# A delta rule and a gated MLP on one core: masks to GpSimd, both grams in one tile, the opening re-ordered, the lanes dealt by TensorE's load

## The chip, the cores and the metric

The kernel runs on one core of a Trainium2 chip. A core has engines that run side by side, each in the order of its own instruction queue: TensorE (PE in the profile; its weight load is PEld), which multiplies matrices into the accumulators PSUM; VectorE (DVE) and ScalarE (ACT), which work element by element and read PSUM; GpSimd (POOL), here used on SBUF alone; and SyncE (SP), which issues most of the DMAs. One engine waits for another by semaphores. The metric is the device time of one execution in microseconds (us), lower is better.

## The reference: what is computed

Inputs are q, k, v of shape (4 batches, 8 heads, 768 steps, 48) and beta (4, 8, 768), all float32, and the weights of a gated MLP. The first half is a recurrence over time, one state of 48 x 48 for each batch and head:

```python
k_n = k / (norm(k, axis=-1) + 1e-6)
state = 0
for t in range(768):
    y[t] = q[t] @ state
    v_old = state.T @ k_n[t]
    state = state + beta[t] * outer(k_n[t], v[t] - v_old)
```

The output y, with its heads side by side, is x of shape (4, 768, 384). The second half is

```python
h = gelu_tanh(x @ w_in)                 # 384 -> 1024
u, v = h[..., :512], h[..., 512:]
v_n = (v - mean(v)) / sqrt(var(v) + 1e-6) * g_ln
v_s = einsum('ts,bsd->btd', w_sg, v_n) + b_sg[:, None]   # mixes the 768 steps
out = x + (u * v_s) @ w_out
```

## The kernel before

**The recurrence in chunks.** Time is cut into 12 chunks of 64 steps (`NCH`, `T`), and six segments of two chunks (`NSEG`). The 32 pairs of batch and head lie as 16 pairs on each half of the partitions. For a chunk, TensorE makes two grams, keys by keys (G) and keys by queries (M). M is masked so that only earlier steps count. From G comes a triangular matrix that must be inverted, Z: its two 32 x 32 diagonal blocks are inverted element by element with 128 blocks side by side, one on each partition (`lanes`, line 301), and the off-diagonal corner is then multiplied together on TensorE (`corner_a`, `corner_b`, lines 435 to 465).

**The lanes.** `gstore` (229) writes G to device memory, `zload` (294) reads a segment's blocks back as `z`. `lanes(s)` gives two lists: `first` (a copy of the diagonal d0 at line 315, a GpSimd select that clears the lower triangle at 316, three Newton steps for 1/sqrt and what follows) and `ops` (a scaling at 338, then rows at 344, outer products and sums at 355 and 362, columns at 349, and a last scaling at 381), all on VectorE. `zstore` (401) writes the result out, makes a transposed copy of half of it on ScalarE (410), writes that too, and its `fetch` reads both back in the layout that TensorE needs, 16 DMAs in all. All these DMAs stand in SP's queue, in program order.

**The chain.** For each chunk c the dictionary of `chain(c)` (504) holds eight steps: `own0/1` (u from Z and v), `old0/1` (less what the state already holds), `state0/1` (the state's update) and `read0/1` (the output), where 0 and 1 are halves of the pairs. Into `old` and `state` the grams of chunk c + 5 are dealt (`gram`, 266; `AHEAD = 5`), into `read` the `keys` (467) of chunk c + 1. `old` opens on a flag: a one-element GpSimd memset (520) that waits for the last matmul of `own`, and for which `old`'s first matmul waits. The values v of a chunk are multiplied by a factor from the keys' norms in `vprep` (489), and `norms` (387) brings those norms into place.

**The MLP.** From chunk 2 on, `Ffn(c - 2)` works on the chunk that is two behind: `turn` (665) transposes x and splits it into a high and a low part (`xh` on ScalarE, `xl` on VectorE, line 678), `value` and `gate` are three matmuls for each product (`mm3`, 648), `moments` (691) and `norm` (696) are the layer norm's sums on VectorE, `scale` and `ustore` finish and store. The weights w_in are float64 words that `decode` (590) takes apart into a high and a low part in three steps `one`, `two`, `three`; there are six blocks of w_in (`decode_win`, 630), which must all be ready before the first `value`. The words of a block come by a DMA on GpSimd's queue (`win_load`, 623). The late weights (w_out by the same `decode`, w_sg by a split) are prepared from chunk 10 on.

**The order.** The engines' order is written out by hand. `tick` (153) takes an operation from the list `bg` (the lanes, later the late weights) and one from `slow`; `tick(n)` calls stand between the steps of the loop over chunks (812 to 945), with fixed numbers. At the end of each even chunk the loop empties what is left of a segment's lanes, stores it, and starts the next list. Before chunk 2 all remaining w_in blocks are decoded in one go (815). After chunk 13 the hand-written order ends, and the last stage (`spatial`, 976; `project`, 995) mixes the steps and projects.

**The opening** (740 to 810): loads of the k and q halves of chunks 0 and 1, keys' grams, q grams, one w_in block in two steps, grams of chunks 2 and 3, lanes(0) in one go, store and fetch, masks, the gram of chunk 4 after the first corner.

**The masks and the factor before:** a ScalarE copy of G out of PSUM, and one VectorE multiplication of M by a constant mask on its way out of PSUM (258, 286); the factor is a VectorE multiplication (492).

## Time and profile before

| what | value |
|---|---|
| time, median of 3 runs | 643.38 us (642.31 to 646.55) |
| the profiled execution, its own time | 636.94 us |
| its span | 634.9 us |
| TensorE, VectorE, ScalarE, GpSimd busy | 471.0, 360.1, 198.1, 66.0 us |
| granted TensorE clock, mean | 0.836 |
| HBM traffic | 55.94 MB read, 29.88 MB written |

All rows below come from one profiled execution, times in us from the start of its span. The profile's chain of waits gives the last stage's matmuls (lines 651 to 653) 27% of the span. A row of a timeline is: start, duration, engine, line, operation, output<-inputs, shape, count, and in brackets how long the engine had been idle and what ended that. A row of a group is: line, engine, operation, tiles, shape, count, then busy us, mean ns of one, and idle us before them with what ended it. A row of stages is explained where it stands.

### The profile page before, as it was taken

Reading aid. Unit: us, or ns where it says so; the run is one execution under the profiler, and the core shown is the slowest. Engines: PE = TensorE matmul, PEld = TensorE weight load, DVE = VectorE, ACT = ScalarE, POOL = GpSimd, SP = SyncE. Lnnn points to the kernel's source line nnn. Section 1 sums busy time; section 2 is a strip of 40 time slices with the busy share of each in tenths; the row PEclk is TensorE's granted clock in tenths of the full one; section 3 lists DMA queues with packets and bytes.
Section 4 is the critical chain, followed back from the end, with each engine's and each line's share of the span. In section 5 each row is a group of like instructions: output and inputs, shape, how many; then the busy total and the mean of one; then the engine's idle time right before and its main releaser. Section 6 shows DMA issues by size and latency. Waiting matters only on the chain. (4 is left out here: it accounts for less than half of the span.)

```text
span 634.9 us, 20005 instructions
## 1 busy us (share of the span) xinstructions
PE 471.0 (74%) x8530; PEld 424.1 (67%) x8531; DVE 360.1 (57%) x1295; ACT 198.1 (31%) x426; POOL 66.0 (10%) x98
## 2 busy tenths in 40 slices
PE   8355656340779595979599691738969999999997
PEld 6352555330567584768488581527859999999997
DVE  1695769878466359647866622753342763633332
ACT  2101213221263435345254451145442331311100
POOL 3100100023000000000000000200000422222210
PEclk9658667675798588879699896777979999999999
DMA  8746864771076957774755655245394664432123
GB/s 157 147 84 167 173 113 118 128 177 66 26 174 128 209 123 180 143 171 104 195 118 149 160 127 138 88 141 140 73 274 118 229 214 152 154 112 93 41 74 113
DMA packets 124872, 87.12 MB, mean 137 GB/s; under 512 B 94352, under 2 KB 110352, under 8 KB 123824
## 3 DMA queue, kind: packets, MB, share of 16 engines
q1 hardware_dynamic: 118336, 81.56, 51.6%
q0 software_dynamic: 864, 3.15, 1.7%
q10 hardware_dynamic: 5584, 1.15, 1.2%
q8 instruction: 67, 1.10, 0.8%
q14 instruction: 21, 0.17, 0.1%
HBM read 55.94 MB, written 29.88 MB: 135 GB/s over the span
## 5 line engine op out<-in xcount | busy, mean ns | idle before, releaser
L72 PE MATMUL ps<-kd 48*64 48x64 f32 (+1 forms) x1024 | 69.9, 306 | 30.2 <-DMA kd<-kqT 28.9
L651 PE MATMUL ps<-winh,xh 128*128 128x512 f32 x72 | 36.2, 503 | 66.4 <-DVE xl L678 56.5
L72 PEld LDWEIGHTS ps<-kd 48*64 48x64 f32 x1024 | 62.1, 182 | 33.4 <-DVE ztmp L355 13.6
L651 PEld LDWEIGHTS ps<-winh,xh 128*128 128x128 f32 x72 | 16.3, 227 | 71.3 <-DVE xl L678 44.1
L355 DVE TENSOR_TENSOR ztmp<-zl 128x72 f32<-128x72 f32 (+13 forms) x228 | 51.6, 262 | 1.5
L362 DVE TENSOR_TENSOR zl<-zl,ztmp 128x72 f32<-128x72 f32 (+13 forms) x228 | 51.0, 260 | 0.0
L988 POOL TENSOR_TENSOR ga<-ga,uT 128x384 f32<-128x384 f32 x32 | 34.4, 1079 | 144.9 <-DVE ga L986 94.8
L72 PE MATMUL ps<-z,kt 64*64 64x64 f32 x704 | 33.0, 260 | 17.3 <-DVE zl L362 9.2
L651 PE MATMUL ps<-xh,winh 128*128 128x256 f32 x144 | 45.3, 314 | 0.4 <-ACT vg L689 0.4
L656 ACT CAST gh<-ga 128x384 fp32r<-128x384 f32 x32 | 16.4, 513 | 86.0 <-POOL ga L988 86.0
L72 PEld LDWEIGHTS ps<-z,kt 64*64 64x64 f32 x704 | 30.1, 171 | 18.1 <-issue 17.6
L652 PE MATMUL ps<-xl,winh 128*128 128x256 f32 x144 | 41.4, 287 | 0.3 <-issue 0.3
L653 PE MATMUL ps<-xh,winl 128*128 128x256 f32 x144 | 41.3, 287 | 0.0
L657 DVE TENSOR_TENSOR gl<-ga,gh 128x384 fp32r<-128x384 f32 x32 | 18.9, 592 | 32.0 <-ACT gh L656 32.0
L286 DVE TENSOR_TENSOR mq<-ps,mask 128x256 f32<-128x256 f32 x32 | 13.5, 422 | 37.6 <-ACT g L285 37.5
L72 PE MATMUL ps<-u,mq 64*64 64x48 f32 x768 | 34.4, 253 | 0.0
L693 DVE BATCH_NORM_STATS2 bs<-vg 128x6 f32<-128x512 f32 x24 | 16.4, 685 | 31.2 <-ACT vg L689 31.2
L651 PEld LDWEIGHTS ps<-xh,winh 128*128 128x128 f32 x144 | 28.2, 196 | 8.2 <-issue 5.4
L652 PE MATMUL ps<-winl,xh 128*128 128x512 f32 x72 | 33.6, 467 | 0.0
L72 PEld LDWEIGHTS ps<-s,w 48*64 48x64 f32 x704 | 25.8, 153 | 11.4 <-issue 5.1
L653 PE MATMUL ps<-winh,xl 128*128 128x512 f32 x72 | 33.4, 464 | 0.0
L72 PEld LDWEIGHTS ps<-u,mq 64*64 64x64 f32 x768 | 31.3, 168 | 2.5 <-issue 1.5
(125 smaller groups left out, 1264.9 us busy)
## 6 DMA issues: line engine op xcount, KB each, us to landing
kd<-kqT SPq DMA_DIRECT2D x20, 384.0 KB, 6.3
vD<-vg SPq DMA_DIRECT2D x48, 128.0 KB, 2.5
uD<-ut SPq DMA_DIRECT2D x48, 128.0 KB, 3.2
vraw<-vD SPq DMA_DIRECT2D x24, 256.0 KB, 3.8
uT<-uD SPq DMA_DIRECT2D x8, 768.0 KB, 5.5
kt<-ktok SPq DMA_DIRECT2D x12, 384.0 KB, 3.8
v<-vtok SPq DMA_DIRECT2D x12, 384.0 KB, 4.3
xD<-x SPq DMA_DIRECT2D x48, 96.0 KB, 2.7
```

The lines of the kernel that those rows point to most:

```text
L72: return nc.tensor.matmul(out=out, lhsT=lhsT, rhs=rhs, start=start, stop=stop, skip_group_check=True)
L286: nc.vector.tensor_tensor(out=M[c % N_M][:, js], in0=st["ps"][:, :, 1], in1=mask.unsqueeze(1).broadcast_to([P, 4, T]), op=ALU.mult)
L355: tv.tensor_tensor(out=st["tmp"][:, at:at + (r1 - r0) * w].rearrange("p (r t) -> p r t", t=w), in0=z[:, r0:r1, i:i + 1].broadcast_to([P, r ...
L362: tv.tensor_tensor(out=z[:, r0:r1, i + 1:32], in0=z[:, r0:r1, i + 1:32], in1=st["tmp"][:, at:at + (r1 - r0) * w].rearrange("p (r t) -> p r ...
L651: nc.tensor.matmul(out=ps, lhsT=sh, rhs=mh, start=(first and i == 0), stop=False)
L652: nc.tensor.matmul(out=ps, lhsT=sh, rhs=ml, start=False, stop=False)
L653: nc.tensor.matmul(out=ps, lhsT=sl, rhs=mh, start=False, stop=(last and i == n - 1))
L656: nc.scalar.copy(out=hi, in_=src)
L657: nc.vector.tensor_tensor(out=lo, in0=src, in1=hi.bitcast(F32), op=ALU.subtract)
L693: nc.vector.bn_stats(out=bs, in_=self.vg[bi])
L988: nc.gpsimd.tensor_tensor(out=ga, in0=ga, in1=uT[:, d], op=ALU.mult)
```

## The change

It does the following. **Masks:** G and M of a chunk share one tile `GM`; ScalarE copies both out of PSUM at once, and GpSimd clears M's upper part by a select in place (`above`, two selects for each half of the pairs, so four a chunk of 64 partitions x 512 elements). **The values' factor** goes to GpSimd, and stands ahead of the corner. **The transposed copy** in `zstore` goes to GpSimd for segments 1 to 5. **In `decode`** the product with the threshold moves from step two to step one and one subtraction goes from VectorE to GpSimd. **The opening:** two w_in blocks are asked for at once and two more after the load of segment 0, the q halves of chunks 0 and 1 after it too; eight of the 18 decode steps run ahead of lanes(0), with step three of a block behind step two of the next; the grams of chunks 2, 3 and 4 are made in the opening with each load two chunks ahead. **The dealing:** every step of TensorE adds its cost from a table `COST` to a clock `pe`, and `spent` takes lane operations in proportion of a span opened when a segment begins; `END` and `BEGIN` say in which chunk and place a segment's lanes must end and the next begin. The ten remaining decode steps are dealt ahead of lanes(2) and emptied before chunk 2. **Late weights:** 22 units at seven places of chunks 10 to 13, each doing step one of a block, step two of the block before and step three of the one before that, with six buffers instead of three.

The diff, cut to its core:

```diff
-    M = [(low if i < 3 else main).tile([P, NP, T], F32, name=f"mq{i}") for i in range(N_M)]
+    GM = [(low if i < 3 else main).tile([P, NP, 2, T], F32, name=f"gm{i}") for i in range(N_M)]
...
+    def above(c, js):
+
+        for sd in range(2):
+            m = GM[c % N_M][TOK[sd], js, 1]
+            nc.gpsimd.affine_select(
+                out=m, in_=m, pattern=[[0, js.stop - js.start], [1, T]], base=0,
+                channel_multiplier=-1, compare_op=ALU.is_gt, fill=0.0)
...
@@ gram
-                mark(nc.scalar.copy(out=g[:, js], in_=st["ps"][:, :, 0]))
-                nc.vector.tensor_tensor(
-                    out=M[c % N_M][:, js], in0=st["ps"][:, :, 1],
-                    in1=mask.unsqueeze(1).broadcast_to([P, 4, T]), op=ALU.mult)
+                mark(nc.scalar.copy(out=GM[c % N_M][:, js], in_=st["ps"]))
+                if qd % 2:
+                    above(c, slice(4 * qd - 4, 4 * qd + 4))
...
@@ zstore
-        nc.scalar.copy(out=zt, in_=z[0:64].rearrange("p s t -> p t s"))
+        (nc.gpsimd.tensor_copy if s else nc.scalar.copy)(out=zt, in_=z[0:64].rearrange("p s t -> p t s"))
...
@@ vprep
-        nc.vector.tensor_tensor(
+        nc.gpsimd.tensor_tensor(
...
@@ decode
         def two():
             nc.scalar.copy(out=hv, in_=ff)
...
+            nc.gpsimd.tensor_tensor(out=ff, in0=ff, in1=hv.bitcast(F32), op=ALU.subtract)
             nc.gpsimd.tensor_tensor(out=lowf, in0=lowf, in1=mf, op=ALU.subtract)
 
         def three():
-            nc.vector.tensor_tensor(out=ff, in0=ff, in1=hv.bitcast(F32), op=ALU.subtract)
...
@@ the opening
+    for k in range(2):
+        win_load(k)
...
+    parts = [decode_win(k) for k in range(2 * NC)]
+    win = parts[0][0:2]
+    for k in range(1, 2 * NC):
+        win += parts[k][0:2] + parts[k - 1][2:3]
+    win.append(parts[-1][2])
+    zload(0)
+    for k in (2, 3):
+        win_load(k)
+    for c in range(2):
+        for sd in range(2):
+            nc.sync.dma_start(out=KD[c][OWN[sd], 1], in_=kqT[c, OWN[sd], 1])
+    tload(0)
+    vload(0)
+    for _ in range(N_EARLY):          # N_EARLY = 8
+        win.pop(0)()
+    first, ops = lanes(0)
+    for op in first:
+        op()
     for c in range(2):
         deal(qgram(c), [])
+        kload(c + 2, 0)
+        kload(c + 2, 1)
+    norms(0)
+    vprep(0)
+    for c in range(2, 5):
+        for phase in gram(c):
+            deal([phase], [])
+        gstore(c, (nc.sync,))
+        if c < 4:
+            kload(c + 2, 0)
+            kload(c + 2, 1)
+        if c == 3:
+            zload(1)
...
+    for op in ops:
         op()
     fetch = zstore(0, nc.scalar)
     fetch()
...
     corner_a(0)
-    tick(12)
+    tick(20)
     corner_b(0)
...
@@ the loop over chunks
+    pe = {"now": 0.0, "from": 0.0, "to": 0.0, "ops": 0}
+    COST = {
+        "own0": 1.1, "own1": 1.1, "old0": 1.0, "old1": 1.0, "state0": 1.0, "state1": 1.0,
+        "read0": 1.2, "read1": 1.2, "turn": 0.8, "value": 2.2, "gate": 1.1, "corner": 0.8}
+    CHUNK = sum(COST.values()) + COST["value"] + 3 * COST["gate"] + COST["corner"]
+
+    def spent(what):
+
+        pe["now"] += COST[what]
+        left = pe["ops"] * max(0.0, (pe["to"] - pe["now"]) / (pe["to"] - pe["from"])) if pe["ops"] else 0
+        while bg and len(bg) > left:
+            tick()
+
+    def span(us):
+        pe.update({"from": pe["now"], "to": pe["now"] + us, "ops": len(bg)})
+
+    END = {1: (1, "corner"), 2: (3, "corner"), 3: (5, "own"), 4: (6, "read"), 5: (8, "read")}
+    BEGIN = {2: (1, "corner"), 3: (3, "corner"), 4: (5, "own"), 5: (7, "own")}
...
         if c == 2:
-            for part in [p for w in win[1:] for p in w]:
-                part()
+            while win:
+                tick()
...
+        def lanes_begin(s):
+            if s >= NSEG:
+                return
+            first, ops = lanes(s)
+            slow.extend(first)
+            if s == 2:
+                def piece():
+                    win.pop(0)()
+                bg.extend([piece] * len(win))
+            bg.extend(ops)
+            span(SPAN.get(s, 1.6) * CHUNK)
...
         if ch:
             gstore(c + AHEAD, (nc.sync,))
-        tick(6)
-        corner_a(c + 1)
+        norms_next()
+        at("corner")
+        vprep(c + 1)
+        corner(corner_a)
...
@@ the late weights
-                raws[k] = raw = wpool.tile([P, half, 2], I32, name="raw", bufs=3)
+                raws[k] = raw = wpool.tile([P, half, 2], I32, name="raw", bufs=6)
...
             def w_unit(k):
+                if k >= 2:
+                    ahead[k - 2][2]()
+                if k >= 1:
+                    ahead[k - 1][1]()
+                ahead.append(w_parts(k))
+                ahead[k][0]()
+                w_fetch(k + 3)
...
+            units = [lambda k=k: w_unit(k) for k in range(n_w + 2)]
```

`at(place)` calls `lanes_end` (the rest of the lanes, `zstore`, `fetch`) and `lanes_begin` where `END` and `BEGIN` name this chunk and place; `unit()` takes one unit of the late weights, after `value(0)`, `old1`, `state0`, `state1`, `gate(2)`, `gate(3)` and `read1`; `w_parts(k)` gives the three steps of `decode` for a block of w_out, and a split followed by two empty steps for one of w_sg.

More of the change, by code (lines that the diff above doesn't have):

```diff
@@ L257, in done @@
             def done():
-                nc.vector.tensor_tensor(
-                    out=M[c % N_M][:, 8 * hf:8 * hf + 8], in0=st["ps"],
-                    in1=mask.unsqueeze(1).broadcast_to([P, 8, T]), op=ALU.mult)
+                nc.scalar.copy(out=GM[c % N_M][:, js, 1], in_=st["ps"])
+                above(c, js)
             return step, done
@@ L506, in chain @@
         z, w, u, v, s, kt, qo, m = (
[L507 removed]
+            t[c % len(t)] for t in (Z, W, U, V, S, KT, QO, GM))
         def evict_u(hf):
@@ L821, in does, with feeds, corner, unit @@
                 ch[name]()
+                spent(name)
+        def feeds(name, *i):
+            if ffn:
+                getattr(ffn, name)(*i)
+                if name in COST:
+                    spent(name)
+        def corner(f):
+            if ch:
+                f(c + 1)
+                spent("corner")
+        def unit():
+            if units:
+                units.pop(0)()
+        def lanes_end(s):
+            while s not in ztile:
+                tick()
+            zstore(s, nc.sync)()
+        def lanes_begin(s):
[9 more added lines that the diff above has]
+            span(SPAN.get(s, 1.6) * CHUNK)
+        def at(place):
+            for s, (cc, p) in END.items():
+                if (cc, p) == (c, place):
+                    lanes_end(s)
+            for s, (cc, p) in BEGIN.items():
+                if (cc, p) == (c, place):
+                    lanes_begin(s)
+        def norms_next():
+            s = (c + 2) // 2
+            if c % 2 == 0 and 1 <= s < NSEG:
+                while s not in ns:
+                    tick()
+                norms(s)
         kload(c + AHEAD + 1, 0)
-        if ffn:
-            ffn.turn()
-        else:
-            tick(8)
+        feeds("turn")
         does("own0")
@@ L830, in delta_rule_gmlp_kernel @@
         kload(c + AHEAD + 1, 1)
-        tick(7)
-        if ffn:
-            ffn.value(0)
-        else:
-            tick(12)
+        at("own")
+        feeds("value", 0)
+        unit()
         does("old0")
```

191 lines of the change are left out of this document (59 added, 132 removed).

## The prediction

> **What bounds the kernel now.** I read the stages first: busy time of each engine in stretches cut at the starts of the chunks. Columns: stretch, its length, then busy us of TensorE (PE), its weight load (PEld), VectorE (DVE), ScalarE (ACT), GpSimd (POOL), granted TensorE clock, DMA share, GB/s.
>
> ```profile
> 106.60:134.00 27.40, 13.20 (x454) 12.23 (x455) 22.98 (x97) 9.22 (x23) 1.39 (x3) 0.57 0.71 148
> 134.00:162.30 28.30, 2.34 (x132) 2.04 (x130) 22.08 (x42) 4.54 (x12) 9.91 (x10) 0.61 0.36 93
> 162.30:354.40 192.10, 157.86 (x4198) 134.13 (x4199) 123.16 (x567) 87.09 (x195) 4.68 (x15) 0.86 0.63 145
> 354.40:381.90 27.50, 22.54 (x603) 19.18 (x605) 10.07 (x38) 12.43 (x25) 0.18 (x2) 0.88 0.64 151
> 381.90:438.20 56.30, 26.13 (x559) 22.32 (x550) 29.91 (x95) 18.35 (x44) 5.14 (x10) 0.67 0.44 123
> 484.00:634.90 150.90, 147.20 (x849) 146.88 (x847) 64.67 (x107) 27.10 (x52) 34.40 (x32) 1.00 0.43 136
> ...
> 333.30:354.40 21.10, 20.04 (x567) 17.34 (x568) 16.20 (x81) 11.24 (x28) 0.18 (x2) 1.00 0.55 139
> ```
>
> Only the last stage is TensorE's own: 147 of 151 us at full clock, and the diff doesn't touch it. Chunks 2 to 8 (162.3 to 354.4) keep neither engine full; chunk 8, the last row, shows what a chunk takes when it runs undisturbed. From 134 to 162 TensorE does 2.3 us of work, and in chunk 10 (381.9 to 438.2) 26 of 56. Then I asked TensorE's groups and its timeline who ended its idle time (in brackets).
>
> ```profile
> L651 PE MATMUL ps<-winh,xh 128*128 128x512 f32 x72 | 36.2, 503 | 66.4 <-DVE xl L678 56.5 <-ACT xh L674 6.9 <-ACT vg L689 3.0
> ...
> 129.61 0.37 PE L72 MATMUL ps<-z,kt 64*64 64x64 f32 x2 [9.18 <-DVE zl L362]
> ...
> 162.25 0.80 PE L651 MATMUL ps<-winh,xh 128*128 128x512 f32 x1 [25.96 <-DVE xl L678]
> ...
> 397.74 0.77 PE L651 MATMUL ps<-winh,xh 128*128 128x512 f32 x1 [13.05 <-DVE xl L678]
> ...
> 430.88 0.34 PE L72 MATMUL ps<-j,ztk 32*32 32x32 f32 x5 [13.10 <-ACT j L448]
> ```
>
> TensorE waits for VectorE's `xl`, a 0.55 us subtraction: it stands on VectorE behind the decode of w_in (162.25), behind the late weights (397.74), and behind what is left of a segment's lanes at each even chunk's end. VectorE, an engine in order, is the bound between the opening and chunk 11.
>
> **Part by part: the opening.** The lanes of one segment are a fixed stretch of VectorE work.
>
> ```profile
> 25.40 0.19 DVE L315 COPY d<-zl 128x32 f32<-128x32 f32 x1 [4.18 <-DMA zl<-gd]
> ...
> 30.15 1.23 DVE L338 TENSOR_TENSOR zl<-zl,nb 128x1024 f32<-128x1024 f32 x1
> ...
> 52.63 1.22 DVE L381 TENSOR_TENSOR zl<-zl,nb 128x1024 f32<-128x1024 f32 x1
> ...
> 64.83 1.51 ACT L465 COPY z<-ps 32x256 f32<-32x256 f32 x4 [1.19 <-PE ps L72]
> ...
> 83.59 0.66 PE L72 MATMUL ps<-kd 48*64 48x128 f32 x2 [5.34 <-DMA kd<-kqT]
> ...
> 105.33 1.23 DVE L381 TENSOR_TENSOR zl<-zl,nb 128x1024 f32<-128x1024 f32 x1
> ...
> 116.56 0.37 ACT L448 COPY j<-ps 128x256 f32<-128x256 f32 x1
> ```
>
> lanes(0): 25.40 to 53.85, 28.4 us, of which 4.7 are its opening steps. What the move to GpSimd costs it is in the next rows: a select ran from 25.66 to 26.93, and VectorE's two-input operation of 0.19 us took 1.12.
>
> ```profile
> 25.66 1.27 POOL L316 TENSOR_SCALAR_AFFINE_SELECT zl<-zl 128x1024 f32<-128x1024 f32 x1 [3.01 <-DVE d L315]
> ...
> 25.84 1.12 DVE L174 SCALAR_TENSOR_TENSOR rsq_t<-d,rsq_y 128x32 f32<-128x32 f32 x1
> ...
> 26.99 0.19 DVE L176 TENSOR_TENSOR rsq_t<-rsq_t,rsq_y 128x32 f32<-128x32 f32 x1
> ...
> 1.22 0.29 POOL masks.py:199 TENSOR_SCALAR_AFFINE_SELECT ident<-ident 128x128 f32<-128x128 f32 x1
> ...
> 21.36 1.29 POOL L609 TENSOR_TENSOR ut<-ut,vg 128x512 f32<-128x512 f32 x1 [15.06 <-DVE ut L607]
> ...
> L988 POOL TENSOR_TENSOR ga<-ga,uT 128x384 f32<-128x384 f32 x32 | 34.4, 1079 | 144.9 <-DVE ga L986 94.8 <-issue 50.1
> L609 POOL TENSOR_TENSOR raw<-raw,m 128x192 f32<-128x192 f32 x8 | 5.0, 628 | 51.7 <-DVE raw L607 49.4 <-issue 2.3
> ```
>
> So a GpSimd operation stops the lanes, all of whose operations read two tiles. A mask is now a select of 512 elements: 0.71 us on the line between 0.29 (128) and 1.27 (1024), four a chunk; VectorE loses between 0 and 0.71 by each. It lost 0.93 of 1.27 above, 0.73 of it; I take 0.6. The values' factor (768 elements, two inputs): 1.29 for 512 and 1.08 for 384 extend to 1.85, of which VectorE loses 1.7; a subtraction of the decode 1.2 of 1.29.
>
> The Trainium skill (SBUF — State Buffer, section "SBUF: two separate sides") calls the ports that the two engines share an exclusive lock, held for the whole instruction against a VectorE operation with two SBUF inputs. By that rule each of 48 selects would cost 0.71 and the sum below would be 5 us higher; the trace agrees that one stops the other, and shows no longer block than the select itself.
>
> Loads: the k halves and two w_in blocks go first, two more follow on GpSimd's queue, the q halves go on SP's behind the load of segment 0. About the same bytes stand ahead of that load (2 MB of w_in where q halves, the load of chunk 2 and one block stood), so it lands as before. Eight decode steps, some 11.6 us, now stand ahead of the lanes and were covered by the 4.18 of idle and more before it; they begin once the words are there. I put lanes(0) 1.1 us later, at 26.5 (0 to 6). All five grams of the opening mask on GpSimd during lanes(0): 20 selects, 12 us; the factor 1.7; two subtractions left over 2.4. It ends at 26.5 + 28.4 + 16.1 = 71.0, against 53.85. The first corner to its last eviction takes 12.5 as before (53.85 to 66.34); the 9.7 of gram 4 and its loads that followed are gone, so chunk 0 starts at 83.5 against 76. The 5.34 wait for kd goes too: its loads are issued two grams ahead.
>
> The queue of lanes(1) is emptied at chunk 0's first step, since no span is open yet; with masks and factor gone nothing stands between, so lanes(1) follows at once: 28.4 + 8 selects 4.8 + factor 1.7 = 34.9, to 105.9, against 106.56. The opening as a whole gains nothing.
>
> **Decode of w_in.** Block to block 6.00 us, of which 1.18 is a wait and 0.68 the subtraction that moves:
>
> ```profile
> 137.41 0.42 DVE L595 TENSOR_SCALAR vg<-ut 128x512 int32<-128x512 int32 x1
> ...
> 140.73 0.68 DVE L612 TENSOR_TENSOR vg<-vg,winh 128x512 f32<-128x512 f32 x1
> ...
> 142.59 0.69 DVE L613 SCALAR_TENSOR_TENSOR winl<-ut,vg 128x512 fp32r<-128x512 f32 x1 [1.18 <-POOL ut L609]
> 143.41 0.43 DVE L595 TENSOR_SCALAR vg<-ut 128x512 int32<-128x512 int32 x1
> ...
> 391.19 0.26 DVE L595 TENSOR_SCALAR m<-raw 128x192 int32<-128x192 int32 x1 [14.13 <-DMA raw<-w_out]
> ...
> 394.12 0.25 DVE L595 TENSOR_SCALAR m<-raw 128x192 int32<-128x192 int32 x1
> ```
>
> Left for chunk 1 are ten steps: 3 x 4.14 + 0.69 = 13.1, with six subtractions that hold VectorE 7.2, the opening steps of lanes(2) 4.7, a factor 1.7 and `xl` 1.1: 27.8. From 105.9 that is 133.7. TensorE is there earlier: corner 2 comes 10 us after the lanes' end (106.56 to 116.56), at 116, and about 12 more bring it to `value` (134.0 less 116.56 less the 9.18, which goes because kt is now asked for ahead of the Z transfers on SP, and an estimated 4 of `turn` and `own`). So 133.7 against 162.25: -28.5.
>
> **Chunks 2 to 8.** VectorE's groups in chunks 3 to 8 (columns: busy, mean ns, idle before and its end):
>
> ```profile
> L693 DVE BATCH_NORM_STATS2 bs<-vg 128x6 f32<-128x512 f32 x12 | 8.2, 680 | 7.1 <-ACT vg L689 7.1
> L286 DVE TENSOR_TENSOR mq<-ps,mask 128x256 f32<-128x256 f32 x16 | 6.8, 424 | 21.3 <-ACT g L285 21.2
> L678 DVE TENSOR_TENSOR xl<-ps,xh 128x384 fp32r<-128x384 f32 x12 | 6.1, 552 | 18.2 <-ACT xh L674 18.2
> L492 DVE TENSOR_TENSOR v<-v,nv 128x768 f32<-128x768 f32 x6 | 5.7, 954 | 6.0 <-DMA v<-vtok 6.0
> ```
>
> Of 123.2 busy, 20 masks (8.4) and 7 factors (6.7) go. About 14 of lanes(2) come in, which were done by 134 (22.98 less opening steps, masks, factor and decode) and now follow the decode. GpSimd stops it 20 x 0.6 + 7 x 1.7 + 4 x 1.0 (the transposed copy, now there) = 28. Sum 150.5. The idle of 21.3 and 6.0 goes with its operations; that of `xl` and the moments, 25.3, stays. 176 against 192.1: -16. ScalarE copies one 512-wide gram where it copied 256, inside its own slack (87 of 192). The flag that opens `old0` and `old1` is a GpSimd memset and now stands behind selects, factor and copy; TensorE's `old` waits for it. I cost it at nothing as long as GpSimd, some 5 us of work a chunk, keeps up. Where lanes must end in the chunk whose corner needs them (1 and 3), the 10 us to the corner are bare; they lie inside VectorE's time.
>
> **Chunks 9 to 13.** Chunk 9 loses the lanes' rest: 20, near chunk 8's 21.1, instead of 27.5: -7.5. Chunk 10: late weights take 2.93 a unit on VectorE (391.19 to 394.12), in three steps 2.1, with two GpSimd subtractions of 0.63 more 3.35; 7 units and 4 of its own: 27 against 56.3, -29.3. The remaining units fit into chunks 11 and 12, where VectorE is mostly idle. Nothing else moves.
>
> Sum: -28.5 - 16 - 7.5 - 29.3 = -81.3, from a span of 634.9 to 553.6. The timed median, 643.38, lies 8.5 above this span (execution 636.94): 562.
>
> **Rivals.** (a) The port costs little. VectorE's blocked 31.5 up to chunk 2 go, chunks 2 to 8 fall to TensorE's 158, chunk 10 to 21: 506. Against it stand the 1.12 us; for it, that narrower selects were never seen against lanes. (b) The two engines go on waiting for each other: VectorE stays at 123.2/192.1 = 64% busy in chunks 2 to 8, so 150.5 take 235, and the time is 621. For it: in-order queues with the same meeting points. Against: 27 us of that idle belonged to operations that left. (c) Slower: the flag. GpSimd gets late, and `old0` and `old1` wait each time as once now:
>
> ```profile
> 108.12 0.35 PE L72 MATMUL ps<-s,w 48*64 48x48 f32 x2 [4.94 <-POOL flag L520]
> ```
>
> 22 flags of 4.94 are 109, so 671; it decides from 3.7 us a flag. For it: the flag there stood behind a 1.27 us select that waited for VectorE; now six operations a chunk do. Against: GpSimd has 20 us a chunk for 5. (d) The spread does nothing, because the lanes end late all the same: that is (b) with its price.
>
> **Chances.** Forecast 0.62 (545 to 590), (a) 0.11, (b) and (d) 0.17, (c) 0.08, 0.02 for (b) with the late weights as slow as now, which is no change. The range reaches into (a) and to (b): 520 to 622. One per cent is what can be told here (the runs spread over 0.7%). Faster by that 0.88 (a few of (b) fall short), the same 0.04, slower 0.08.
>
> **What would show it.** VectorE two-input operations of a microsecond beside selects; lanes(0) ending near 71; the first `value` near 134 with VectorE busy up to it; chunk 10 below 30; `old` without waits for the flag. Wrong if lanes(0) ends before 60 (the port), or if VectorE is under 75% busy in chunks 2 to 8 (waiting).

## The result and the profile after

The changed kernel takes 614.75 us (median of 4, 614.02 to 616.54) where the kernel before takes 642.85 (median of 4, 642.27 to 646.55): a ratio of 0.956, 95% interval 0.951 to 0.960. The forecast was 562, so 28 of the 81 us came. The profiled execution took 614.38 us, its span is 612.7. Medians and ratios below leave out executions over 1.5% slower than the fastest of the same kernel.

The stages of the changed kernel, cut where the prediction cut those of before (length, busy us of PE, PEld, DVE, ACT, POOL, granted clock, DMA share, GB/s):

```profile
97.90:139.30 41.40, 18.86 (x671) 16.86 (x663) 21.97 (x51) 10.10 (x22) 16.44 (x17) 0.66 0.63 130
139.30:342.00 202.70, 158.20 (x4199) 134.82 (x4200) 144.95 (x623) 84.68 (x194) 37.04 (x46) 0.87 0.61 140
342.00:369.10 27.10, 21.73 (x572) 19.02 (x571) 4.72 (x18) 10.61 (x24) 1.65 (x3) 0.91 0.54 124
369.10:400.20 31.10, 24.90 (x574) 21.61 (x573) 18.02 (x45) 11.61 (x29) 7.94 (x13) 0.77 0.54 151
400.20:423.50 23.30, 19.96 (x321) 17.35 (x320) 12.64 (x41) 10.10 (x24) 4.09 (x8) 0.82 0.50 126
423.50:461.80 38.30, 25.13 (x134) 22.15 (x133) 18.03 (x60) 17.27 (x35) 0.00 (x0) 0.78 0.55 160
461.80:612.70 150.90, 147.18 (x849) 146.86 (x847) 65.19 (x107) 27.04 (x51) 34.37 (x32) 1.00 0.44 136
```

Set against the forecast, stage by stage (the stages of before that the prediction doesn't show, chunk 11 and chunks 12 and 13, are 438.2 to 455.6 and 455.6 to 484.0 of its span):

| stage | before | forecast | after | after less forecast |
|---|---|---|---|---|
| to the first `value` matmul | 162.3 | 133.7 | 139.3 | +5.6 |
| chunks 2 to 8 | 192.1 | 176 | 202.7 | +26.7 |
| chunk 9 | 27.5 | 20 | 27.1 | +7.1 |
| chunk 10 | 56.3 | 27 | 31.1 | +4.1 |
| chunk 11 | 17.4 | 17.4 | 23.3 | +5.9 |
| chunks 12 and 13 | 28.4 | 28.4 | 38.3 | +9.9 |
| last stage | 150.9 | 150.9 | 150.9 | 0 |

Two stages bring the whole gain: the opening with the decode (-23.0) and chunk 10 (-25.2). Chunks 2 to 8 became 10.6 longer in these two profiles, not 16 shorter, and the chunks after 10 lost 15.8 for which the prediction had no term. How far a stage moves between profiles of the same program has to be known first: chunks 2 to 8 are the same in the changed kernel and in the runs e1, e8 and e9 below, and took 202.7, 199.3, 195.8 and 202.8 us. So a difference of a few us in one profile of this stage shows nothing.

In chunks 2 to 8 VectorE does what the prediction said, 145 us with the lanes of segment 2 in it, but it is no longer what TensorE stands for. What ended TensorE's waits there before the change, then after it with VectorE's longest (us in total, times, longest; `issue` is a wait for which the profile shows no releaser):

```profile
PE ps L651 <- DVE xl L678: 39.8, 4, 26.0
PE ps L72 <- issue: 16.0, 13, 4.3
PE ps L72 <- DMA kt<-ktok: 3.6, 1, 3.6
```

```profile
PE ps L73 <- issue: 25.8, 13, 6.4
PE ps L73 <- DMA z<-zd: 15.2, 4, 9.3
PE ps L652 <- DVE xl L679: 6.6, 1, 6.6
...
DVE xl L679 <- ACT xh L675: 39.7, 6, 10.7
```

The longest wait for `xl`, 26.0 before and 6.6 after, is the one that ends at the stage's first matmul. Inside the stage TensorE waited 13.8 us for `xl` before the change and not at all after it. In place of that stand 15.2 us for z, where there was none, and 9.8 more of `issue`.

Two of the longest `issue` waits (5.0 and 6.4 us), and one of 4.2 in chunk 9, are the start of `read`, into which the next chunk's `keys` are dealt, and they need kt. SyncE's queue and TensorE's timeline show the first (start, length, engine, line):

```profile
244.72 1.92 SPq L417 DMA_DIRECT2D z<-zd  x4
...
251.94 3.00 SPq L425 DMA_DIRECT2D ztk<-ztd  x4
255.04 0.39 SPq L129 DMA_DIRECT2D v<-vtok  x1
255.53 0.38 SPq L129 DMA_DIRECT2D kt<-ktok  x1
...
259.93 0.46 PE L73 MATMUL ps<-z,kt 64*64 64x64 f32 x3 [4.96 <-issue]
```

Sixteen fetches of one solved segment, of which the rows show the first and the last four, hold SyncE's queue for 10 us; v and kt of the chunk stand behind them, and TensorE goes on 4.4 us after kt's issue. By the page of the profile, kt lands 4.0 us after its issue (the median). So the place "10 us to the corner" of the prediction was not the only one that went bare: whatever is queued behind the fetches is late too.

SyncE also stands still itself in these chunks, and what is queued behind waits with it:

```profile
SPq L716 <- ACT vg L713: 28.6, 5, 8.7
...
SPq L417 <- DMA zd<-zl: 12.4, 4, 5.4
```

The first is the store of the MLP's scaled v, which waits for the scale step; it was 12.5 us in the same chunks before, and the change moved the scale step behind the last gate and the reads in every chunk. The second is the fetch waiting until the solved block's store has landed (5.5 before). No run put the scale step of chunks 2 to 8 back, so its share in the late loads is not known.

Chunk 1 shows what follows from it on the other engines:

```profile
111.29 2.28 SPq L234 DMA_DIRECT2D gd<-gm  x4
113.67 0.46 SPq L407 DMA_DIRECT2D zd<-zl  x1
...
119.23 1.29 PE L73 MATMUL ps<-z,gm 32*32 32x32 f32 x64 [8.59 <-DMA z<-zd]
...
120.63 0.37 ACT L446 COPY j<-ps 128x256 f32<-128x256 f32 x1 [8.99 <-PE ps L73]
120.90 0.62 ACT L603 CAST winh<-vg 128x512 fp32r<-128x512 f32 x1
...
124.15 0.69 DVE L611 SCALAR_TENSOR_TENSOR winl<-wraw,vg 128x512 fp32r<-128x512 f32 x1 [18.67 <-POOL wraw L608]
...
139.28 0.79 PE L652 MATMUL ps<-winh,xh 128*128 128x512 f32 x1 [6.63 <-DVE xl L679]
```

The block of lanes(1) was solved at 97.97, but its store stands on SyncE behind the store of a gram that is made later (the diff puts it there: `at("corner")` comes after `gstore`), and goes at 113.67. TensorE's corner waits for it until 119.23, ScalarE stands on the corner's copy, the decode's cast stands behind that copy on ScalarE, GpSimd's subtraction needs the cast, and VectorE stands 18.67 us on the subtraction. The 27.8 us of VectorE's work between the lanes and `xl` took 41.3.

### The profile page after: what moved, and what is told of

The parts are those of the page before. It is cut to its first block, busy times and chain, and to the rows that moved or that the text cites. A ratio compares the mean times of both kernels' runs of the same rounds, so it can differ in the third digit from the quotient of the medians.

```text
span 612.7 us, 19739 instructions
## 1 busy us (share of the span) xinstructions
PE 477.3 (78%) x8403; PEld 429.2 (70%) x8403; DVE 370.4 (60%) x1229; ACT 199.1 (32%) x429; POOL 140.6 (23%) x174
## 4 chain that ended last, share of the span: by engine, by line
PE 58%; DVE 15%; issue 9%; DMA 7%; SPq 5%; ACT 4%; POOL 1%; ACTq 0%; POOLq 0%; DVEq 0%
PE ps L73 18%; PE ps L652 14%; PE ps L654 13%; PE ps L653 12%; DMA zd<-zl 2%; DVE ztmp L353 2%; DMA vraw<-vD 2%; DVE zl L360 1%; DVE zl L342 1%; DVE rsq_t L175 1%; DMA ztk<-ztd 1%; SPq L417 1%; DMA kd<-kqT 1%; PE ps L674 1%; SPq L737 1%
## 5 line engine op out<-in xcount | busy, mean ns | idle before, releaser
L73 PE MATMUL ps<-kd 48*64 48x128 f32 (+1 forms) x896 | 63.9, 306 | 21.6 <-DMA kd<-kqT 18.0
L73 PEld LDWEIGHTS ps<-kd 48*64 48x64 f32 x896 | 56.8, 170 | 24.0 <-DMA kd<-kqT 14.5
L360 DVE TENSOR_TENSOR zl<-zl,ztmp 128x72 f32<-128x72 f32 (+13 forms) x228 | 56.2, 282 | 0.0
L243 POOL TENSOR_SCALAR_AFFINE_SELECT gm<-gm 64x512 f32<-64x512 f32 x48 | 33.3, 694 | 97.4 <-ACT gm L284 96.0
L679 DVE TENSOR_TENSOR xl<-ps,xh 128x384 fp32r<-128x384 f32 x24 | 12.2, 552 | 66.4 <-ACT xh L675 66.4
L73 PE MATMUL ps<-u,gm 64*64 64x48 f32 x768 | 37.4, 262 | 0.0
L284 ACT COPY gm<-ps 128x512 f32<-128x512 f32 x40 | 23.5, 587 | 39.2 <-PE ps L73 39.2
L73 PEld LDWEIGHTS ps<-u,gm 64*64 64x64 f32 x768 | 33.6, 176 | 1.7 <-issue 0.4
L73 PE MATMUL ps<-s,qo 48*64 48x48 f32 x704 | 26.3, 228 | 9.0 <-issue 7.4
L490 POOL TENSOR_TENSOR v<-v,nv 128x768 f32<-128x768 f32 x12 | 18.3, 1528 | 64.1 <-DMA v<-vtok 61.6
```

Source lines behind the costliest of these rows:

```text
L73: return nc.tensor.matmul(out=out, lhsT=lhsT, rhs=rhs, start=start, stop=stop, skip_group_check=True)
L243: nc.gpsimd.affine_select(out=m, in_=m, pattern=[[0, js.stop - js.start], [1, T]], base=0, channel_multiplier=-1, compare_op=ALU.is_gt, fi ...
L284: mark(nc.scalar.copy(out=GM[c % N_M][:, js], in_=st["ps"]))
L360: tv.tensor_tensor(out=z[:, r0:r1, i + 1:32], in0=z[:, r0:r1, i + 1:32], in1=st["tmp"][:, at:at + (r1 - r0) * w].rearrange("p (r t) -> p r ...
L490: nc.gpsimd.tensor_tensor(out=V[c % N_2], in0=V[c % N_2], in1=nvs[c // 2][:, c % 2].unsqueeze(2).broadcast_to([P, NP, HD]), op=ALU.mult)
```

## Experiments

Every run stands in this table by its median, its ratio to the runs of before on the same chip (95% interval; the two kernels that leave work out have none), and by three stages of its profile: the first `value` matmul, the length of chunks 2 to 8, and what is left of the span from TensorE's first transpose of chunk 11 (197.3 before the change).

| run | median us | ratio | first `value` | chunks 2 to 8 | from chunk 11's start |
|---|---|---|---|---|---|
| the change | 614.75 | 0.956 (0.951 to 0.960) | 139.3 | 202.7 | 212.9 |
| e1_end1 | 614.48 | 0.963 (0.931 to 0.994) | 142.6 | 199.3 | 210.0 |
| e2_end2 | 616.68 | 0.966 (0.932 to 1.000) | 137.9 | 204.0 | 213.6 |
| e3_no_select | 605.71 | | 136.5 | 196.7 | 212.4 |
| e4_kt_ahead | 604.34 | 0.947 (0.919 to 0.974) | 137.5 | 199.5 | 212.9 |
| e5_loads_ahead | 604.33 | 0.948 (0.937 to 0.959) | 140.9 | 197.3 | 212.3 |
| e6_loads_and_z_ahead | 595.04 | 0.933 (0.924 to 0.942) | 131.8 | 200.4 | 211.0 |
| e7_more_vector | 607.62 | 0.955 (0.943 to 0.967) | 139.3 | 198.6 | 211.1 |
| e8_end_order | 617.80 | 0.969 (0.959 to 0.979) | 137.8 | 195.8 | 223.7 |
| e9_two_units | 617.78 | 0.967 (0.962 to 0.971) | 137.7 | 202.8 | 206.9 |
| e10_scale_early | 606.67 | 0.950 (0.942 to 0.957) | 142.3 | 200.1 | 210.7 |
| e11_z_first | 591.03 | 0.924 (0.919 to 0.928) | 131.6 | 195.4 | 210.1 |
| e12_late_by_hand | 594.07 | 0.931 (0.924 to 0.937) | 131.2 | 190.6 | 214.5 |
| e13_no_loads | 575.98 | | 137.2 | 175.7 | 210.7 |
| e14_loads_gpsimd | 596.25 | 0.934 (0.923 to 0.945) | 137.7 | 193.8 | 210.4 |
| e15_all | 586.35 | 0.915 (0.909 to 0.921) | 132.6 | 190.2 | 209.8 |

The stages of e10 come from an execution of 614.01 us, and their lengths are not compared with those of other runs. Kernels that are the same up to the first `value` have it between 137.7 and 139.3 (the change, e7, e8, e9), and those that are the same from chunk 11 on take 210.0 to 213.6 there (the change, e1 to e7).

### The place of the fetches, or the port

**e1_end1** and **e2_end2** store and fetch a solved segment earlier, **e3_no_select** takes GpSimd's masks away.

```diff
-    END = {1: (1, "corner"), 2: (3, "corner"), ...     # e1: 1: (1, "own")
+    END = {1: (1, "own"), 2: (3, "corner"), ...        # e2: 2: (2, "read"), and SPAN = {2: 1.05}
 def gram(c), done():
-                if qd % 2:
-                    above(c, slice(4 * qd - 4, 4 * qd + 4))   # e3, and the same call in qgram
```

> One edit to the changed kernel: segment 1's lanes end, and its Z is stored and fetched, at chunk 1's own step instead of at its corner. Place theory (the missing gain is Z stored too late on SyncE's queue, with TensorE and, behind the corner's copy, ScalarE and the decode waiting for it): the 8.6 us wait before chunk 1's corner falls below 2, the 18.7 us hole in VectorE's decode closes, the first value matmul comes 8 to 15 us earlier than 139.3, the time falls by 7 to 14 us to 601 to 608. Port theory (the missing gain is GpSimd holding up VectorE): the decode's operations keep their length, the time changes by less than 3 us.

> One edit to the changed kernel: segment 2's lanes end, and its Z is stored, at chunk 2's read step instead of chunk 3's corner (with its span shortened to 1.05 chunks so that they are dealt by then). Place theory: the 9.3 us wait for Z before chunk 3's corner goes, up to 3 us come back as a longer chunk 2, the time falls by 5 to 9 us to 606 to 610. Port theory: the same work on VectorE, no change beyond 3 us.

> The 48 selects on GpSimd are left out, so the queries' grams are not masked (that part of the computation is missing); nothing else changes. Port theory: VectorE gets 0.6 us for each back, 12 in lanes(0), 5 in lanes(1), 12 in chunks 2 to 8, and the time falls by 20 to 30 us to 585 to 595. Place theory: lanes(0) ends 8 to 12 us earlier and that alone is seen, chunks 2 to 8 stay within 4 us of 202.7, and the time falls by 6 to 12 us.

e1 and e2 moved a wait each and gained nothing. In e1 the wait of 8.59 us at chunk 1's corner fell to 2.17 (for z's transposed copy) and one of 6.83 came a few steps later; VectorE's hole stayed, with another engine at its root. First GpSimd and VectorE of e1, then TensorE of e1, then TensorE of e2:

```profile
122.31 1.48 POOL L490 TENSOR_TENSOR v<-v,nv 128x768 f32<-128x768 f32 x1 [8.43 <-DMA v<-vtok]
...
127.53 1.74 DVE L611 SCALAR_TENSOR_TENSOR winl<-wraw,vg 128x512 fp32r<-128x512 f32 x1 [19.66 <-POOL wraw L608]
...
123.65 0.46 PE L73 MATMUL ps<-z,kt 64*64 64x64 f32 x2 [6.83 <-DMA gd<-gm]
```

```profile
193.46 0.46 PE L73 MATMUL ps<-z,kt 64*64 64x64 f32 x2 [11.20 <-DMA kt<-ktok]
```

With the fetches earlier, v's load stands behind them; GpSimd, in order, stands on v's factor with the decode's subtractions behind it. At chunk 3 of e2 the wait for z is gone, but kt now stands on SyncE behind the fetches and the MLP's twelve stores, and TensorE waits 11.20 for it.

e3 shortened lanes(0) from 40.4 us to 31.1 (25.81 to 56.88) for its 20 selects, 0.47 us each, where the prediction took 0.6; the span of its one profile is 8.7 us shorter (612.7 to 604.0). The port's price was near enough; nothing like the missing 53 us lies there. In chunks 2 to 8 VectorE was busy 10.3 us less (the columns are those of the stages above):

```profile
136.50:333.20 196.70, 157.12 (x4198) 134.96 (x4199) 134.66 (x623) 84.49 (x194) 23.72 (x26) 0.87 0.61 143
```

and the stage, 196.7, stayed among the lengths of the changed program (195.8 to 202.8). The Trainium skill (SBUF — State Buffer, section "SBUF: two separate sides") calls the shared pair an exclusive lock held for a whole instruction, the other engine being blocked. The trace agrees that an operation is held up, but the loss is smaller than a whole select: beside eight selects in a row (0.70 us each) VectorE's operations come one to a select and take 0.68 us instead of 0.19, so 0.49 is lost by each. The rows of the changed kernel, VectorE and GpSimd in lanes(0):

```profile
29.04 5.64 POOL L243 TENSOR_SCALAR_AFFINE_SELECT gm<-gm 64x512 f32<-64x512 f32 x8
...
26.07 1.27 DVE L313 COPY d<-zl 128x32 f32<-128x32 f32 x1
...
29.79 0.68 DVE L177 TENSOR_TENSOR rsq_t<-rsq_t,rsq_y 128x32 f32<-128x32 f32 x1
30.50 0.68 DVE L178 SCALAR_TENSOR_TENSOR rsq_y<-rsq_t,rsq_y 128x32 f32<-128x32 f32 x1
...
65.25 1.22 DVE L379 TENSOR_TENSOR zl<-zl,nb 128x1024 f32<-128x1024 f32 x1
...
L243 POOL TENSOR_SCALAR_AFFINE_SELECT gm<-gm 64x512 f32<-64x512 f32 x48 | 33.3, 694 | 97.4 <-ACT gm L284 96.0
```

**e4_kt_ahead** asks for kt a chunk sooner, ahead of everything that holds SyncE's queue.

```diff
-        if c > 0:
-            tload(c + 1)
+        tload(c + 2)
```

> One edit to the changed kernel: the keys by token (kt) of a chunk are asked for one chunk earlier; there are three buffers for them. Place theory in its second half (loads stand behind Z's 19 transfers and the stores on SyncE's queue): TensorE's waits of 5.0, 6.4 and 4.2 us before the keys in chunks 5, 7 and 9 fall below 2 each, and the time falls by 6 to 14 us to 601 to 609, less what the next late load (queries, values) takes. Port theory: no change beyond 3 us.

The waits at `read` are gone (chunk 9 takes 21.3 us instead of 27.1) and the median is 10 us lower, though the intervals of the two ratios overlap; the waits for z are left as they were. So the theory became: **after the change SyncE's in-order queue gates TensorE.**

### Is VectorE the bound at all, and what do the loads cost

```diff
 e5: at the top of chunk c, ahead of at("own"); the later calls go
+        tload(c + 2)
+        if c > 0:
+            vload(c + 1)
+            qload(c + 1)
 e6: e5, and
-    END = {1: (1, "corner"), 2: (3, "corner"), 3: (5, "own"), ...
+    END = {1: (1, "own"), 2: (3, "own"), 3: (4, "read"), ...     # BEGIN of the next segments alike
 e7: the change, and behind each of the four gates
+            if 2 <= c <= 8:
+                nc.vector.tensor_tensor(out=busy, in0=winl[:, 0, 0:512]..., in1=winl[:, 1, 0:512]..., op=ALU.add)
```

> All of chunk c+1's loads (v, qo) and kt of chunk c+2 are issued at the top of chunk c, ahead of the 19 transfers of a Z block; nothing else is changed. Theory Queue (what gates TensorE after the change is SyncE's in-order queue: a load that stands behind the 19 transfers or the stores comes late): the kt waits go as in the kernel with kt alone ahead (604.3 us), and at chunk 1 the decode's hole (18.7 us of idle VectorE) shrinks because GpSimd no longer stands on v; the three Z waits of 7 to 8.5 us stay. 598 to 605 us, value later than 130. Theory VectorE (the forecast's own: in chunks 2 to 8 the time is VectorE's work): a load that comes earlier changes nothing while VectorE is the bound, 612 to 617 us.

> As the kernel with all loads ahead, and the lanes' solved blocks are stored and fetched earlier too: at 'own' of chunks 1 and 3 and at 'read' of chunk 4 in place of the corner of chunks 1 and 3 and 'own' of chunk 5, each next segment begun at the same place. Theory Queue: the waits for z (7.9, 8.4 and 7.0 us) go as well, with nothing left to take their place but VectorE, which must deliver sooner: 580 to 594 us. Theory VectorE: the lanes must end sooner while VectorE has the same work, so the wait becomes one for the lanes: 600 to 615 us.

> The changed kernel with four more two-input operations on VectorE in each of chunks 2 to 8 (128x512, f32 in, bf16 out, result not used), 28 in all, some 0.6 us each by the row of a 128x512 two-input operation: about 17 us more VectorE work, 145 to 162 us of the 203 us of these chunks. Theory VectorE (it is the bound there): +14 to +18 us, 629 to 633. Theory Queue (it is not; it waits for xl while TensorE waits for transfers): the extra work goes into VectorE's idle time, 0 to +5 us, 614 to 620.

e7 is the plain answer to the prediction's bound. The stage and the added operations in e7:

```profile
139.30:337.90 198.60, 158.62 (x4199) 136.13 (x4200) 166.86 (x651) 84.64 (x194) 41.43 (x46) 0.86 0.60 142
...
L856 DVE TENSOR_TENSOR busy<-winl 128x512 bf16<-128x512 f32 x28 | 22.5, 803 | 0.1
```

VectorE was given 22.5 us more and is 84% busy, and the stage, 198.6, lies among those of the unchanged program (195.8 to 202.8); the ratio is the change's own, 0.955. With e3, VectorE's work was varied by -10 and +22 us, and the stage followed neither. The amount of VectorE's work does not bound chunks 2 to 8. Theory VectorE falls.

e5 gained what e4 did and no more: v and qo early gave nothing beyond kt. e6 gained 9 more, all of it before the first `value` (131.8): with v's load and z both early, VectorE has no idle stretch over 2 us left before it, where e5 still had one of 18.66. In chunks 2 to 8 it gained nothing, 200.4: the wait for z at chunk 3 was still 9.3 us, since z's store now stood behind the loads that had been put first.

**e11_z_first** orders the queue by need: the two stores of the solved block, v, the fetches, and then qo, kt, kd.

```diff
 e11: e6, the scale step of e10 (below), and
-        at("own")
+        at("own", lambda: vload(c + 1) if c > 0 else None)   # runs between zstore and its fetches
+        if c > 0:
+            qload(c + 1)
+        tload(c + 2)
+        kload(c + AHEAD + 1, 0)                              # no longer at the top of the chunk
+        kload(c + AHEAD + 1, 1)
```

> The kernel with loads and Z ahead (595.0 us), and at 'own' the solved block's two stores are issued first, then v's load, then the 16 fetches, and only then qo, kt and kd (kd no longer at the chunk's top); with the scale step of chunks 10 to 13 as in the run beside it. Theory Queue: z's store no longer lands behind 2 MB of loads, the waits of 3.3 and 9.3 us for z go and the decode's hole shrinks, the scale step gives its 7 to 11: 573 to 585 us. Rival Bytes (what a chunk loads takes the transfers' time whatever the order): z comes early but kd, kt or qo come late in its place; only the scale step gains: 584 to 592.

591.0: the rival's figure, and not clearly less than e6 (the intervals of the ratios overlap). The waits for z fell from 9.4 to 2.1 us in the stage, and `issue` waits stayed (24.4 to 24.6). The stage took 195.4 at a granted clock of 0.90, where e6's took 200.4 at 0.86; e12, the same program in these chunks, took 190.6. That late loads took the place of the late z is the reading that fits; no row names what the `issue` waits stood for.

### Order or bytes

Two kernels tell apart whether the loads are late by their place in SyncE's queue or by the time their bytes take. **e13_no_loads** leaves them out, **e14_loads_gpsimd** issues the same bytes from GpSimd's queue.

```diff
 e13: in tload, vload, qload
-        if c < NCH:
+        if c < 3:
 e14: in tload, vload, qload, from chunk 3 on
-            paced(KT[c % N_K], ktok[c])                      # nc.sync
+            paced(KT[c % N_K], ktok[c], nc.gpsimd)
 e15: e11 and e14
```

> The changed kernel with the loads of kt, v and qo left out from chunk 3 on (4 transfers, 1.2 MB a chunk; the chunks compute on the values of an earlier chunk, so the output isn't the reference's). It bounds what these loads cost in any way, by SyncE's order or by bytes. If loads are behind TensorE's waits in chunks 2 to 8 (waits for kt, qo and the unexplained 'issue' waits, 25.8 us): chunks 2 to 8 fall from 202.7 to 178 to 188 us, the run to 588 to 598. If the waits are Z's own path and the chain xh, xl: only the 10 us that kt alone gave, 602 to 607.

> The changed kernel with the same loads issued from GpSimd's queue from chunk 3 on, the same bytes at the same places of the program. Theory Order (the loads are late because they stand in SyncE's order behind 19 transfers and the stores): within 5 us of the run without these loads. Theory Bytes (they are late because transfers of the chunk share the DMA engines): within 4 us of the changed kernel, 610 to 618. If GpSimd standing on a load's pacing wait delays masks and factor instead: 616 to 630.

> The kernel with Z first (591.0 us) with the loads of kt, v and qo issued from GpSimd's queue, as in the run that did that alone (596.3 us, 18.5 less than the changed kernel, with its three waits of 7.9 to 11.9 us for z still there). If what the two gave is different time (the one Z's place on SyncE's queue, the other the loads' place): 574 to 584 us. If it is the same time (both only take SyncE's backlog away, and the bytes stay): 586 to 593 us, with chunks 2 to 8 at 188 to 195 us.

Chunks 2 to 8 of e13, e14 and e15, each with its waits of TensorE for z and `issue`:

```profile
137.20:312.90 175.70, 149.72 (x4199) 127.66 (x4200) 145.06 (x623) 84.51 (x194) 38.01 (x46) 0.94 0.52 115
...
PE ps L73 <- DMA z<-zd: 14.7, 4, 7.9
PE ps L73 <- issue: 9.7, 13, 1.9
```

```profile
137.70:331.50 193.80, 154.93 (x4198) 132.73 (x4199) 148.41 (x623) 84.53 (x194) 53.01 (x74) 0.88 0.64 146
...
PE ps L73 <- DMA z<-zd: 23.5, 3, 11.9
PE ps L73 <- issue: 13.9, 12, 3.2
```

```profile
132.60:322.80 190.20, 155.97 (x4202) 132.61 (x4200) 141.89 (x605) 84.45 (x194) 53.39 (x75) 0.89 0.69 156
...
PE ps L73 <- issue: 21.4, 13, 4.7
...
PE ps L73 <- DMA z<-zd: 3.1, 2, 2.9
```

Without the loads the stage takes 175.7 us, 27 less than the changed kernel's profile and 20 less than the shortest of the same program (e8), with the same work on VectorE. `issue` waits fall from 25.8 to 9.7: 16 us of the unnamed waits were the loads'. Of the 27 us, 18.5 are idle time of TensorE (44.5 to 26.0) and 8.5 its own busy time (158.2 to 149.7, the same 4199 matmuls at a clock of 0.94 instead of 0.87).

The same bytes from another queue (e14) take 18 us from the whole run's median, which lies between the figures of Theory Order and Theory Bytes. In this stage they give 8.9 of the 27 (193.8), or 2.0 if e8's profile is the measure; e15 gives 12.5 or 5.6 (190.2), and e12, which leaves the loads on SyncE in e11's order, is as short (190.6). So order is worth some of what the loads cost in this stage, at most about half, and single profiles don't fix the share. 14.5 us stay with every order that was tried, and the loads' bytes on the DMA engines (0.69 of them busy in e15, against 0.52 without the loads) are what e13 takes away beyond the order; which part of it is transfers that share the engines, and which is the clock that fell, no run separates. The Trainium skill (DMA: Bandwidth & Descriptors, section "Issuing engines are not separate DMA queues") says that issuing from several engines saves only the issuing sequencer's time, usually small beside the transfer itself, since all run on the same 16 engines. That the transfers go on meeting each other agrees with the 14.5. That the saving is small is not what this case shows, where the queue that issues also waits: 18 us by the medians, 14 by the ratios.

e15, at 586.35 us and 0.915 of before (0.909 to 0.921), is faster than both kernels: 4.3% under the changed one by the ratios. The run and its stage have the figures of "the same time": what e11 and e14 took away was largely one backlog.

### The chunks after the tenth

The changed kernel's ScalarE and TensorE at the start of chunks 12 and 13:

```profile
427.78 0.62 ACT L657 CAST vnh<-vraw 128x512 fp32r<-128x512 f32 x1 [3.85 <-DMA vraw<-vD]
428.31 1.51 ACT L713 ACTIVATE vg<-vg,mr,rsq_y 128x512 f32<-128x512 f32 x2
429.73 0.83 ACT L675 CAST xh<-ps 128x384 fp32r<-128x384 f32 x2
...
446.79 1.52 ACT L713 ACTIVATE vg<-vg,mr,rsq_y 128x512 f32<-128x512 f32 x2 [2.85 <-DVE mr L705]
...
430.24 0.80 PE L652 MATMUL ps<-winh,xh 128*128 128x512 f32 x1 [6.43 <-ACT xh L675]
...
448.73 0.79 PE L652 MATMUL ps<-winh,xh 128*128 128x512 f32 x1 [6.74 <-ACT xh L675]
```

`xh`, for which TensorE stands, is behind the scale step of the chunk before, which the change moved behind the last gate and the reads; and that stands at chunk 12 on the last stage's split of vraw, at chunk 13 on `mr`, the end of the Newton steps. Before the change the waits for `xh` at the start of chunks 12 and 13 were 1.1 and 5.7. Three runs took one suspect away each.

```diff
 e8:  the hand-written order is kept to the end of the last stage's first loads and splits
-    by_hand.close()
     ...
     fetch_u(0, 1)
+    by_hand.close()
 e9:  in unit()
-            if units:
+            for _ in range(min(2, len(units))):
 e10:
         corner(corner_b)
+        if c >= 10:
+            ffn.scale()
         feeds("gate", 3)          # and no scale at the end of these chunks
```

> The order written out by hand is kept up to the last stage's first loads and splits (fetch of v and u for batch 0), so that no split of vraw stands on ScalarE ahead of chunk 12's and 13's scale and xh. Theory Order (chunks 12 and 13 are 9.9 us longer than before the change because ScalarE, in order, stands on a vraw transfer with xh behind it): TensorE's waits of 6.4 and 6.7 us for xh shrink to under 3 each, chunks 11 to 13 become 5 to 9 us shorter; the splits now stand in front of the last stage and give back 2 to 6 of it: 605 to 613 us. Rival (the late units themselves fill ScalarE and VectorE in these chunks, whatever stands between): the waits stay within 2 us of what they were, 613 to 618.

> The changed kernel with two late-weight units at each place in place of one, so that they end near the middle of chunk 11 and chunks 12 and 13 hold none. Theory Scale (chunks 11 to 13 are longer than before the change because the scale step, with twelve Newton operations in front of it, now stands after the chunk's last matmuls, and the next chunk's xh and xl stand behind it): the waits of 6.4 and 6.7 us at the start of chunks 12 and 13 stay above 5 us each; chunk 10 grows by 2 to 8 us, 612 to 620. Theory Units (the late units on ScalarE and VectorE make chunks 12 and 13 long): both waits fall below 3 us and chunks 11 to 13 lose 6 to 10 us; 604 to 611.

> The changed kernel with the scale step of chunks 10 to 13 back in front of the last gate, where it stood before the change; nothing else. Theory Scale: the waits for xh at the start of chunks 11, 12 and 13 (3.3, 6.4, 6.7 us) fall to under 2.5 us each, chunks 11 to 13 lose 7 to 11 us, 603 to 608 us where the changed kernel takes 614.5. Theory Units: the waits stay within 2 us of what they were, 612 to 617.

e8: the waits for `xh` stayed (5.0 and 6.5 us), and the last stage began with a wait of its own,

```profile
459.32 0.69 PE L652 MATMUL ps<-wsgh,vnh 128*128 128x384 f32 x1 [13.18 <-ACT vnh L657]
```

so the splits between the chunks were worth having, and the time from chunk 11's start rose from 212.9 to 223.7. With no split of vraw in front, `xh` stood there behind a scale step that waited for `mr` (2.9 and 3.2 us). e9: chunk 10 grew from 31.1 to 42.8 us, what followed fell by 6.1 (206.9), and the waits for `xh` at chunks 12 and 13 were 1.6 and 7.4: one is Theory Units' figure, the other Theory Scale's. e10: the wait at chunk 12 fell to 3.7, the one at chunk 13 rose to 9.2 (3.7 and 9.3 in e11, which has the scale step early too). The split of vraw now holds it:

```profile
444.77 0.62 ACT L657 CAST vnh<-vraw 128x512 fp32r<-128x512 f32 x1 [3.28 <-DMA vraw<-vD]
```

**e12_late_by_hand** is e11 with the last stage's first loads at the top of chunk 12 and its splits by hand behind the gates of chunks 12 and 13.

> The kernel with Z first (591.0 us, scale early in chunks 10 to 13), and the last stage's first loads and splits are put by hand into chunks 12 and 13: the vraw loads at the top of chunk 12, the splits of vnh behind the gates, so that none stands on ScalarE in front of xh with its transfer still under way. Theory Both (in chunks 12 and 13 either of two things holds xh: the scale step with its Newton operations in front of it, or a split that waits for vraw; taking one away leaves the other): the waits for xh there, 3.7 and 9.3 us in the kernel with Z first, fall under 2.5 us each and the last stage begins without a wait for vnh over 4 us; 578 to 585 us. Rival Scale alone (the early scale has given what there is, the rest moves to the last stage's start, as the 13.2 us wait for vnh did where the order was kept by hand with the late scale): 588 to 593 us.

It gained nothing (594.1 against 591.0, the ratios' intervals overlap): the wait at chunk 13 became 13.6, and another transfer was at its root, one of the late weights that was now behind the last stage's loads:

```profile
416.79 0.51 ACT L657 CAST wsgh<-raw 128x384 fp32r<-128x384 f32 x1 [8.11 <-DMA raw<-w_sgT]
...
424.56 0.79 PE L652 MATMUL ps<-winh,xh 128*128 128x512 f32 x1 [13.60 <-ACT xh L675]
```

What the scale step's place costs is not shown: e11 and e15, which have it early, take 210.1 and 209.8 us from chunk 11's start, and the kernels with it late 210.0 to 213.6. Shown is that late weights that reach into chunks 11 to 13 cost 3 to 7 us of the 15.8 there (e9's 206.9, for which chunk 10 pays more), and that in each version that was tried ScalarE's order puts something that waits in front of `xh`: the scale step behind `mr` (e8), a split behind vraw (e10), a split of a late weight behind its load (e12). An order in which none waits was not found, so the rest is not shown to be one cause.

## Why the prediction was wrong

**The step that failed** is "VectorE, an engine in order, is the bound between the opening and chunk 11", carried into "Chunks 2 to 8" as a sum of VectorE's work and idle time. Its work was sized about right, 150.5 us forecast (the terms as printed add up to 150.1) and 145 measured; the idle time that was to stay, 25.3, became 57.8, of which 39.7 are VectorE's own waits for `xh`. e7 adds 22.5 us to VectorE and e3 takes 10.3 away, both for nothing in this stage. What TensorE waits for in its place are transfers, and no load had a term in the sum: without kt, v and qo the stage takes 175.7 (e13). That this is the forecast's 176 is luck, since that kernel leaves out loads the forecast kept, and VectorE is idle for 31 us in it. The stage of before already held what the sum left out: TensorE's 16.0 us of `issue` waits and 3.6 for kt were counted as VectorE's shadow. The waits for `xl` went as forecast (13.8 us inside the stage); the others stayed, and the fetches that the change moved into chunks 1, 3 and 5 put 10 us of SyncE's queue in front of v and kt, and waits for z where there were none.

**"the 10 us to the corner are bare; they lie inside VectorE's time"** failed in chunk 1. The corner's copy stands on ScalarE in front of the decode's cast, so VectorE could not work on beside the wait: a hole of 18.67 us. The first `value` came at 139.3 for 133.7 in spite of lanes that ended 8 us sooner than forecast. Earlier z alone (e1) didn't close the hole, since GpSimd then stood on v; z and v together moved `value` to 131.8 (e6), 2 below the forecast.

**The opening** went as worked out, with the port mis-sized: lanes(0) began at 26.07 (26.5 forecast) and ended at 66.47 (71.0). The 20 selects cost 9.3 us and not 12 (the prediction took 0.6 for each where its own row, 0.73 of 0.71, gave 0.52), and the factor with the subtractions cost 2.6 and not 4.1, since only one subtraction still ran when the lanes began. The factor itself took 2.08 us there, and 1.53 on the mean, where 1.85 was expected; the two rows that the prediction extended give 1.71 on a straight line. The end lay between the two conditions that the prediction named for it, nearer to its own.

**Chunk 9**: 20 was forecast and 27.1 measured, and 21.3 once kt was ahead (e4). The mechanism, the end of the lanes' rest, was right; the wait for kt hid it.

**Chunk 10**: -25.2 for -29.3. The stage came out as the prediction said, and this is the largest gain of a stage; no run takes the spread of the three steps away alone. Part of it is work that moved: chunks 10 to 13 together went from 102.1 to 92.7, 9.4 less. Late weights finished sooner (e9) cost chunk 10 11.7 us and gave back 6.1.

**"Nothing else moves"** failed in chunks 11 to 13, +15.8. The scale step is an instruction group that the diff moves past the last gate and the reads, and the late units now reach into these chunks; the prediction followed neither in ScalarE's order. It had costed edits by the engine that they load, and the moved scale step loads none: it changes what stands in front of `xh`, and on SyncE what stands behind its store.

**Of the rivals**, (b) came nearest. Its number is 621 and its mechanism, engines that wait for each other at the same meeting points, was the right one, except that SyncE's queue and the loads are among what they meet at. The nearness of the number is partly luck: it puts 59 us into chunks 2 to 8, where 26.7 of the miss lie, and nothing into the chunks after 10. VectorE was 71.5% busy in the stage, 145 of 202.7, which is the condition under which the prediction called itself wrong. (a) falls with e3, which has no select and still takes 605.7, and (c) with TensorE's waits in chunks 2 to 8: no flag is among them.

## What to carry to other kernels

An engine that is idle a third of a stage is the bound only if taking work from it, or giving it more, moves the time: twenty microseconds of idle work on the suspect is a cheap test, and belongs ahead of a sum that is made of its busy time. A queue that issues transfers is an engine in order like the others: when a block of issues is moved, list what stands behind it, when each of those is needed, and order the queue by need; a moved wait comes back at the next item. Before a stage's change is read, see how far the stage moves between profiles of the same program, here 7 us of 200. For a step that is moved, look at what it is now in front of on every engine that it touches, even where its own cost is nothing.

## What was not expected of the hardware

- Sixteen fetches of 32 and 64 KB held SyncE for 10.2 us (244.72 to 254.94), 0.64 us each, so a block of small transfers is a wait of its own for whatever is behind it, however few its bytes.
- Without the loads of kt, v and qo, the same 4199 matmuls took 149.7 instead of 158.2 us of busy time, at a granted clock of 0.94 instead of 0.87 (e13), with 26.0 us of idle time instead of 44.5. If the waits lowered the clock, a wait of TensorE costs twice; that is inferred from these two profiles, and no run changed the clock alone.
- A copy of a transposed view on GpSimd, 64x1024, took 1.96 us (five of them, 9.8 us), where a select over 128x1024 took 1.27.
